# Local attention on 64-row matmul tiles, one score bank per head, with the order of the program redone

## The chip, the cores and the metric

The kernel runs on one core of a Trainium2 chip. The metric is the device time of one execution in microseconds (us); less is better. The engines are named as the profile names them: PE is the matmul engine and PEld its weight loads, DVE, ACT and POOL are the vector, scalar and GpSimd engines, and SP issues the DMAs.

## The reference

Batch 4, 8 heads, 576 positions, 64 channels. Each head gets a full attention over positions averaged by fours, and a local attention in which a position sees only those less than 4 away. Their sum goes through two feed-forward stages.

```python
def _attn_ref(q, k, v):
    ...
    out_d = sm_attn(q_d, k_d, v_d)            # on means of 4 positions
    out_up = np.repeat(out_d, factor, axis=2)
    mask = np.abs(pos[:, None] - pos[None, :]) < factor
    scores = scale * np.matmul(q, k.transpose(0, 1, 3, 2))
    scores = np.where(mask, scores, -1000000000.0)
    scores = scores - np.max(scores, axis=-1, keepdims=True)
    attn = np.exp(scores)
    attn = attn / (np.sum(attn, axis=-1, keepdims=True) + 1e-09)
    out_local = np.matmul(attn, v)
    return (out_up + out_local).astype(np.float32)

def reference(**kwargs):
    ...
    x = np.ascontiguousarray(attn_out.transpose(0, 2, 1, 3)).reshape(B, S, H * D)
    x = _moe_ref(x=x, **moe_kwargs)           # x @ w_in, relu, conv of 3, gate, @ w_out
    return _moe2_ref(x=x, **moe2_kwargs)      # low-rank mix of positions, @ w_ch1, relu, @ w_ch2
```

## The kernel before

The 32 heads are worked off as 16 pairs, two heads of 64 channels on 128 rows. For a pair, q and k are loaded by position (words alq, alk), turned on PE (aqT, akT), and copied out of PSUM by ACT or DVE (aqc, akc). The 576 queries are cut into ten blocks of 58; block i sees the 64 keys that start at KS[i]. Two neighbouring blocks share an instruction's output: block 2j stands on rows 0 to 57, block 2j+1 on rows 64 to 121.

- Scores (emit_S, L449 and L453): one matmul writes the mask into a PSUM tile and one matmul for each block adds q k to it. The tile kbd holds k with the other head's half as zeros, so that 128 rows and 128 moving columns give both heads' scores at once. The five pairs of blocks are split into three (S0) and two (S1), one PSUM tile each.
- Softmax: DVE takes the maxima (emit_M, L460), ACT the exponentials (emit_E, L471), POOL or DVE divides (emit_norm, L514).
- The probabilities are turned on PE (emit_T, L526) and copied into the tile PT (emit_Tc, L542). PT keeps two heads apart and has zeros off its diagonal, so each PSUM tile needs four copies of 64 rows: a head's rows times a block's columns.
- Product with v (emit_PV, L562): for each pair of blocks and each head one matmul over 128 rows, the keys of both blocks, and 116 moving columns. The tile vw holds v by block pair.
- The averaged attention runs beside it (Sd L480, turned probabilities L530, product L573), and emit_x (L594) adds both.

The first feed-forward stage has units of 12 matmuls (g1, L805) and 9 (g2, L867), the second g3 (L974) and g4 (L993); all read pairs of high and low parts. The weights arrive as 64-bit numbers and are decoded (L213 to L220), split (L225) and completed (L229) on ACT, DVE and POOL. Three tiles w1t, in turn, receive the first stage's weights.

Nothing schedules: the string SEQ is the order, a list of words that are emitted one by one. Each engine takes its instructions in that order, so a waiting instruction holds up all behind it on its engine. The PSUM tiles of the attention come from four buffers used in turn (tag "st"). Products of the first stage begin at the word 1.0, when four pairs have gone through; the other pairs are interleaved with the products.

Of the kernel before, what the change touches and what calls it, by code (L numbers as in the profile page):

```python
# [8 lines left out]
F32 = mybir.dt.float32  # L9
# [3 lines left out]
AF = mybir.ActivationFunctionType  # L13
# [8 lines left out]
    SEQ="alk.0 alq.0 alv.0 akT.0 aks.0 aqT.0 aqsv.0 lc C aqc.0 akc.0 wl.0 aS0.0 aS1.0 aM0.0 aE01.0 aM1.0 wd.0 "  # L22
# [143 lines left out]
def mixer_kernel(ctx, tc, q, k, v, w_in, conv_w, w_out, mU, mV, w_ch1, w_ch2, out, stop=9, dbg=None, early_end=False):  # L166
# [5 lines left out]
    nc = tc.nc  # L172
# [106 lines left out]
    for i in range(2):  # L279
        nc.gpsimd.memset(PT[64 * i:64 * i + 64, :, :, 1 - i], 0.0)  # L280

# [787 lines left out]
```

## Time and profile before

| | us |
|---|---|
| median of 3 runs | 804.06 (803.35 to 804.09) |
| the profiled execution | 803.76 |
| its span on the core | 802.0 |
| PE busy | 761.0 (95%) |
| DVE busy | 447.5 (56%) |
| ACT busy | 357.2 (45%) |
| POOL busy | 190.3 (24%) |

The busy shares are means over stages that differ, so the views by stretch of time come first. Matmul records overlap: the time that a group of matmuls takes is read from the start of its row to the start of the next row, not from the mean duration of one. A matmul on 32-bit operands that are not turned leaves two records, so a row with x20 stands for ten matmuls; a transpose or a matmul of the feed-forward stages leaves one.

### The profile page before, as it was taken

The page shows a single profiled execution, that of the slowest core. Times are in us where ns is not written, and L with a number is a line of the kernel's source. Part 1 is how long each engine was busy: PE and PEld are TensorE (multiplying, and loading weights), DVE is VectorE, ACT ScalarE, POOL GpSimd, SP SyncE. Part 2 cuts the span into 40 slices and gives each one's busy share as a digit, 9 for nine tenths or more (in the row PEclk, how much of TensorE's full clock was granted, in tenths as well). Part 3 has the DMA queues.
Part 4 walks back from the last instruction along what each step waited for, and adds up shares of the span by engine and source line. Part 5 has one row for each costly group of instructions (what it writes and reads, how often), then busy time and mean ns, then how long its engine had stood idle before and what let it go on. Part 6 is the DMA issues. An engine that isn't in the chain of part 4 may idle for free.

```text
span 802.0 us, 12065 instructions
## 1 busy us (share of the span) xinstructions
PE 761.0 (95%) x4421; PEld 666.4 (83%) x4421; DVE 447.5 (56%) x879; ACT 357.2 (45%) x1077; POOL 190.3 (24%) x266
## 2 busy tenths in 40 slices
PE   4576999999999999999999999999999999999998
PEld 3455788888888788987899999999999989999997
DVE  6887988788988878898986711121221112122112
ACT  3777887887776665767453311111111111111110
POOL 5356566455415242143610000000000000000000
PEclk9578999999999999999999999999999999999999
DMA  6878564333232113111133210010010001001001
GB/s 153 194 177 197 117 123 95 81 93 101 72 85 74 44 56 103 53 54 54 52 120 121 75 40 0 1 40 1 1 39 1 1 1 40 0 1 40 1 1 39
DMA packets 85967, 50.98 MB, mean 64 GB/s; under 512 B 63228, under 2 KB 80404, under 8 KB 85908
## 3 DMA queue, kind: packets, MB, share of 16 engines
q1 hardware_dynamic: 85908, 50.21, 24.0%
q8 instruction: 35, 0.57, 0.3%
q14 instruction: 24, 0.20, 0.1%
HBM read 45.47 MB, written 4.72 MB: 63 GB/s over the span
## 4 chain that ended last, share of the span: by engine, by line
PE 85%; DVE 7%; ACT 3%; DMA 2%; POOL 1%; issue 1%; SPq 0%; DVEq 0%; POOLq 0%; ACTq 0%
PE acc L993 25%; PE g L974 13%; PE gb L974 13%; PE acc L867 11%; PE g L805 9%; PE S L453 2%; PE gb L805 2%; PE O L562 2%; PE tr L359 1%; DMA w1t<-in_moe_w_out_dram 1%; PE h L901 1%; PE T L526 1%; PE ut L960 1%; PE Sd L480 1%; DVE hc L841 1%
## 5 line engine op out<-in xcount | busy, mean ns | idle before, releaser
L993 PE MATMUL acc<-w,a 128*128 128x512 f32 x864 | 216.6, 394 | 0.0
L993 PEld LDWEIGHTS acc<-w,a 128*128 128x128 f32 x864 | 160.8, 188 | 29.0
L867 PE MATMUL acc<-w,ghl 128*128 128x512 f32 x432 | 117.5, 401 | 0.4 <-DVE ghl L858 0.3
L974 PE MATMUL g<-uT,w 128*128 128x384 f32 x576 | 111.9, 339 | 0.0
L974 PE MATMUL gb<-uT,w 128*128 128x384 f32 x576 | 111.3, 339 | 0.0
L974 PEld LDWEIGHTS gb<-uT,w 128*128 128x128 f32 x576 | 101.9, 188 | 3.8
L974 PEld LDWEIGHTS g<-uT,w 128*128 128x128 f32 x576 | 101.9, 188 | 3.8
L983 DVE SCALAR_TENSOR_TENSOR a<-gb,a 128x384 fp32r<-128x384 f32 x48 | 26.7, 557 | 124.7 <-ACT a L982 124.7
L983 DVE SCALAR_TENSOR_TENSOR a<-g,a 128x384 fp32r<-128x384 f32 x48 | 26.7, 557 | 124.5 <-ACT a L982 124.5
L805 PE MATMUL g<-xhl,w 128*128 128x386 f32 (+1 forms) x456 | 95.2, 347 | 0.0
L867 PEld LDWEIGHTS acc<-w,ghl 128*128 128x128 f32 x432 | 77.6, 188 | 16.5 <-issue 2.5
L982 ACT ACTIVATE a<-g 128x384 fp32r<-128x384 f32 x48 | 23.6, 492 | 136.1 <-PE g L974 127.9
L805 PEld LDWEIGHTS g<-xhl,w 128*128 128x128 f32 x456 | 79.2, 189 | 3.8 <-issue 1.7
L982 ACT ACTIVATE a<-gb 128x384 fp32r<-128x384 f32 x48 | 23.6, 491 | 130.0 <-PE gb L974 126.2
L841 DVE SCALAR_TENSOR_TENSOR hc<-hc,cw 128x384 f32<-128x384 f32 x96 | 65.0, 682 | 11.3 <-ACT hc L835 9.2
L471 ACT ACTIVATE P<-S,nm 122x64 f32<-122x64 f32 x160 | 48.1, 319 | 10.6 <-DVE nm L460 10.4
L858 POOL TENSOR_TENSOR ghl<-hc,ghl 128x384 fp32r<-128x384 f32 x24 | 26.1, 1088 | 83.6 <-ACT ghl L855 73.5
L471 ACT ACTIVATION_READ_ACCUMULATOR P<-S,nm 122x1 f32 x160 | 33.7, 211 | 0.0
L453 PE MATMUL S<-kbd,qT 128*58 128x128 f32 x320 | 28.6, 315 | 5.2 <-DVE kbd L414 5.2
L855 ACT ACTIVATE ghl<-hc 128x384 fp32r<-128x384 f32 x48 | 25.1, 523 | 18.8 <-DVE hc L850 17.1
L850 DVE SCALAR_TENSOR_TENSOR hc<-hc 128x384 f32<-128x384 f32 x48 | 30.3, 633 | 5.6 <-ACT hc L845 5.0
L845 ACT ACTIVATE hc<-hc 128x384 f32<-128x384 f32 x48 | 24.9, 524 | 17.9 <-DVE hc L841 17.7
(131 smaller groups left out, 1076.4 us busy)
## 6 DMA issues: line engine op xcount, KB each, us to landing
wraw<-in_moe_w_ch_dram SPq DMA_DIRECT2D x29, 512.0 KB
kr<-in_k_dram SPq DMA_DIRECT2D x32, 144.0 KB
qr<-in_q_dram SPq DMA_DIRECT2D x32, 144.0 KB
vr<-in_v_dram SPq DMA_DIRECT2D x32, 144.0 KB
out_dram<-u SPq DMA_DIRECT2D x17, 256.0 KB
w1t<-in_moe_w_in_dram SPq DMA_DIRECT2D x8, 512.0 KB
w1t<-in_moe_w_out_dram SPq DMA_DIRECT2D x8, 512.0 KB
vw<-in_v_dram SPq DMA_DIRECT2D x64, 64.0 KB
```

The source lines that it names most:

```text
L453: nc.tensor.matmul(ps[64 * a:64 * a + QB, j], e["qT"][:, QB * i:QB * i + QB], e["kbd"][:, :, KS[i]:KS[i] + W], start=False, stop=j == n - 1)
L471: nc.scalar.activation(out=e["P"][:, i, h], in_=ps[:122, j, h], func=AF.Exp, bias=e["nm"][:, i, h:h + 1], accum_out=e["sm"][:, i, h:h + 1])
L805: nc.tensor.matmul(p[:, :wd], w[:, a, cc], xhl[g, cc][:, b, :wd], start=k == 0, stop=k == 3 * NCC - 1)
L841: nc.vector.scalar_tensor_tensor(out=o, in0=inner(g, hts[n], k), scalar=cw[:, k * NF + f:k * NF + f + 1], in1=o, op0=ALU.mult, op1=ALU.add)
L850: nc.vector.scalar_tensor_tensor(out=o, in0=o, scalar=1.0, in1=inner(g, hts.pop(n), 1), op0=ALU.add, op1=ALU.mult)
L855: nc.scalar.activation(out=t[:, 0], in_=cts[n], func=AF.Copy)
L858: eng.tensor_tensor(ghl[n][:, 1], cts.pop(n), ghl[n][:, 0].bitcast(F32), op=ALU.subtract)
L867: nc.tensor.matmul(acc[g][c], t[:, a, c * P:(c + 1) * P], w[:, b], start=f == 0 and i == 0, stop=f == NF - 1 and i == 2)
L974: nc.tensor.matmul(p[:, :TB], w[:, a, cc], uT[g, cc][:, b, :TB], start=k == 0, stop=k == 3 * NCC - 1)
L982: nc.scalar.activation(out=t[:, 0], in_=p[:, :TB], func=AF.Relu)
L983: nc.vector.scalar_tensor_tensor(out=t[:, 1], in0=p[:, :TB], scalar=0.0, in1=t[:, 0].bitcast(F32), op0=ALU.max, op1=ALU.subtract)
L993: nc.tensor.matmul(acc2[g][c], t[:, a, c * P:(c + 1) * P], w[:, b], start=f == 0 and i == 0, stop=f == NF2 - 1 and i == 2)
```

## The change

- kbd becomes kT: k of both heads on 128 rows without zeros; one copy for a PSUM tile where there were two (emit_kc).
- emit_S makes one PSUM tile for each head (five block pairs by 64 keys). A matmul now uses 64 rows, the head's channels, and 64 moving columns; 20 matmuls a pair where there were 10. emit_M and emit_E go by head.
- PT loses its zeros and its split by head and block: the turned probabilities stand as the transposes left them, a head's keys on 64 rows, and are copied whole (emit_Tc): one copy where there were four.
- emit_PV uses 64 rows and 58 moving columns; 20 matmuls a pair where there were 10. The two heads' outputs stay in one PSUM tile, head 0 on rows 0 to 63 and head 1 on rows 64 to 127. vw is loaded by block, head h on rows 64h and on, with six DMAs a pair in place of eight.
- SEQ is written anew.

```diff
-    SEQ="alk.0 alq.0 alv.0 akT.0 aks.0 aqT.0 aqsv.0 lc C aqc.0 akc.0 wl.0 aS0.0 aS1.0 aM0.0 aE01.0 aM1.0 wd.0 "
+    SEQ="wl.2 wd.2 lc C wd.2 wd.2 wl.0 wd.2 wd.0 wh.2 alk.0 wd.0 wd.0 wd.0 wh.0 alq.0 aqT.0 wo.0 alv.0 avd.0 "
...
-        t = p0.tile([P, 2, S], F32, name=f"kbd{i}")
-        nc.gpsimd.memset(t, 0.0)
-        kbds.append(t)
+        kTs.append(p0.tile([P, S], F32, name=f"kT{i}"))
...
-    PT = pa.tile([P, 2, 5, 2, QB], F32, name="PT")
-    for i in range(2):
-        nc.gpsimd.memset(PT[64 * i:64 * i + 64, :, :, 1 - i], 0.0)
+    PT = pa.tile([P, 5, 122], F32, name="PT")
...
-        vw = st[p]["vw"] = pa.tile([P, 5, 2, D], F32, name="vw", tag="vw")
+        vw = st[p]["vw"] = pa.tile([P, 10, D], F32, name="vw", tag="vw")
...
         for c, src in e["kps"]:
-            for h in range(2):
-                rows = slice(64 * h, 64 * h + 64)
-                engines[h](like(kbd[rows, h, c], src), src[rows])
+            copy(like(e["kT"][:, c], src), src)
...
-        n = SB[m].stop - SB[m].start
-        ps = e["S", m] = ps0.tile([P, n, 2, W], F32, name="S", tag="st")
-        nc.tensor.matmul(ps, identR, mask[:, SB[m]].unsqueeze(2).to_broadcast([P, n, 2, W]), start=True, stop=False)
-        for j in range(n):
+        for h in range(2):
+            e["S", h] = ps0.tile([P, 5, W], F32, name="S", tag="st")
+            nc.tensor.matmul(e["S", h], identR, mask, start=True, stop=False)
+        for j in range(5):
             for a in range(2):
-                i = 2 * (SB[m].start + j) + a
-                nc.tensor.matmul(ps[64 * a:64 * a + QB, j], e["qT"][:, QB * i:QB * i + QB],
-                                 e["kbd"][:, :, KS[i]:KS[i] + W], start=False, stop=j == n - 1)
+                i = 2 * j + a
+                for h in range(2):
+                    rows = slice(64 * h, 64 * h + 64)
+                    nc.tensor.matmul(e["S", h][64 * a:64 * a + QB, j], e["qT"][rows, QB * i:QB * i + QB],
+                                     e["kT"][rows, KS[i]:KS[i] + W], start=False, stop=j == 4)
...
-            for h in range(2):
-                for a in range(2):
-                    (copy2 if a and copy2 else copy)(PT[64 * a:64 * a + 64, h, SB[m], a], src[64 * h:64 * h + 64, :, 64 * a:64 * a + QB])
+            copy(PT[:, SB[m]], ps[:, :122 * n].rearrange("p (i x) -> p i x", i=n))
...
-            c = 2 * QB * (i % 4)
-            for h in range(2):
-                nc.tensor.matmul(O[64 * h:64 * h + 64, c:c + 2 * QB], e["vw"][:, i, h],
-                                 PT[:, h, i].rearrange("p a x -> p (a x)"), start=True, stop=True)
+            for a in range(2):
+                c = 2 * QB * (i % 4) + QB * a
+                for h in range(2):
+                    rows = slice(64 * h, 64 * h + 64)
+                    nc.tensor.matmul(O[rows, c:c + QB], e["vw"][rows, 2 * i + a], PT[rows, i, 64 * a:64 * a + QB],
+                                     start=True, stop=True)
```

Three places show what the new order does. In these rows a number behind the shape counts instructions in a row; L numbers are those of the kernel that the rows are from. First PE among the products, with the scores of one pair (S), turned probabilities (T), products with v (O<-PT) and the averaged attention's (O<-PTd). Before:

```order
L805 MATMUL g<-xhl,w_583 128x386 x12
L449 MATMUL S<-mask,identR 128x384
L453 MATMUL S<-kbd_128,qT_132 58x128 x6
L449 MATMUL S<-mask,identR 128x256
L453 MATMUL S<-kbd_128,qT_132 58x128 x4
L526 MATMUL T<-ident,P 128x122 x3
L530 MATMUL T<-ident,Pd 72x96 x4
L805 MATMUL g<-xhl,w_724 128x386 x6
L867 MATMUL acc<-w_431,ghl 128x512 x3
L562 MATMUL O<-PT,vw 64x116 x2
L867 MATMUL acc<-w_431,ghl 128x512 x6
```

PE among the products now:

```order
L855 MATMUL acc<-w_287,ghl 128x512 x3
L441 MATMUL S<-mask,identR 128x320 x2
L447 MATMUL S<-kT_133,qT_136 58x64 x20
L355 MATMUL tr<-ident,qr 128x96 x3
L520 MATMUL T<-ident,Pd 72x96 x4
L793 MATMUL g<-xhl,w_683 128x386 x6
L355 MATMUL tr<-ident,kr 128x96 x3
L793 MATMUL g<-xhl,w_683 128x386 x6
L855 MATMUL acc<-w_287,ghl 128x512 x3
L355 MATMUL tr<-ident,kr 128x96 x3
L551 MATMUL O<-PT,vw 64x58 x20
L562 MATMUL O<-PTd,vd 64x144 x4
```

A pair's scores are one group of 20 small matmuls behind both masks, where they were two groups with a mask ahead of each, and its products with v are here one group of 20, followed by the averaged attention's, which keep 72 rows.

Second, ACT before the products begin: the copies of the turned probabilities (PT), of k (kbd, kT), exponentials (P, Pd) and weights (w1t, w). Before:

```order
L471 ACTIVATE P,sm<-S,nm 122x64 x6
L213 ACTIVATE w1t<-w1t 128x512
L542 COPY PT<-T 64x3x58 x4
L471 ACTIVATE P,sm<-S,nm 122x64 x2
L225 ACTIVATE w_360<-w1t 128x512
L471 ACTIVATE P,sm<-S,nm 122x64 x2
L213 ACTIVATE w1t<-w1t 128x512
L414 COPY kbd_128<-tr 64x576 x2
```

ACT before the products now:

```order
L407 COPY kT_133<-tr 128x576
L489 ACTIVATE Pd,smd<-Sd,nmd 96x144 x3
L461 ACTIVATE P,sm<-S,nm 122x64 x2
L529 COPY PT<-T 128x366
L376 ACTIVATE qT_136<-tr 128x576
L213 ACTIVATE w1t<-w1t 128x512
L225 ACTIVATE w_658<-w1t 128x512
```

Four copies of 64 rows have become one of 128, and two copies of k have become one.

Third, the first DMAs that SP issues: k, q and v of the first pairs (kr, qr, vr) and weights (w1t, craw). Before:

```order
L298 DMA kr<-in_k_dram 96x6x64 x2
L298 DMA qr<-in_q_dram 96x6x64 x2
L320 DMA vr<-in_v_dram 72x2x256 x2
L700 DMA craw<-in_moe_conv_w_dram 24x256
L329 DMA w1t<-in_moe_w_in_dram 128x4x256
L327 DMA w1t<-in_moe_w_out_dram 128x1024
```

SP's first DMAs now:

```order
L325 DMA w1t<-in_moe_w_in_dram 128x4x256
L688 DMA craw<-in_moe_conv_w_dram 24x256
L325 DMA w1t<-in_moe_w_in_dram 128x4x256
L295 DMA kr<-in_k_dram 96x6x64 x2
L295 DMA qr<-in_q_dram 96x6x64 x2
L316 DMA vr<-in_v_dram 72x2x256 x2
```

Two weight blocks of 512 KB now stand ahead of the first pair's k and q.

## Rows read from the trace of the kernel before

**Rows 1.** Stretches: busy us (instructions) by engine, PEclk, DMA share, GB/s.

```profile
core 0: us, PE busy (x) PEld busy (x) DVE busy (x) ACT busy (x) POOL busy (x), PEclk, DMA share, GB/s
0.00:88.00 88.00, 55.39 (x410) 44.18 (x410) 70.75 (x136) 61.40 (x227) 47.34 (x76) 0.79 0.75 176
93.00:280.00 187.00, 186.83 (x1397) 156.10 (x1398) 159.15 (x373) 141.16 (x520) 89.25 (x134) 1.00 0.35 84
280.00:400.00 120.00, 115.70 (x571) 101.99 (x570) 105.42 (x172) 77.58 (x164) 46.46 (x50) 1.00 0.20 62
400.00:802.00 402.00, 398.30 (x2020) 359.99 (x2018) 108.06 (x188) 72.09 (x142) 5.79 (x4) 1.00 0.08 28
```

**Rows 2.** Chain that ended last, front: start us, us, what.

```profile
60.09 4.60 DMA w1t<-in_moe_w_out_dram
...
70.86 6.59 DMA w1t<-in_moe_w_out_dram
```

**Rows 3.** Waits of the DMA queue, 0 to 88 us: total, times, longest.

```profile
SPq L327 <- POOL w L229: 16.3, 4, 7.8
```

**Rows 4.** Timeline of PE, untiled and score matmuls: start us, us, instruction.

```profile
118.95 0.87 PE L453 MATMUL S<-kbd,qT 128*58 128x128 f32 x12
119.75 0.39 PE L449 MATMUL S<-mask,identR 128*128 128x256 f32 x1
120.07 0.65 PE L453 MATMUL S<-kbd,qT 128*58 128x128 f32 x8
120.65 0.53 PE L526 MATMUL T<-ident,P 122*128 122x122 f32 x3
...
241.10 0.37 PE L526 MATMUL T<-ident,P 122*128 122x122 f32 x2
241.31 0.33 PE L530 MATMUL T<-ident,Pd 96*72 96x96 f32 x2
```

**Rows 5.** Timeline of PE, products with v and their neighbours.

```profile
123.21 0.42 PE L562 MATMUL O<-PT,vw 128*64 128x116 f32 x4
123.56 1.66 PE L867 MATMUL acc<-w,ghl 128*128 128x512 f32 x6
...
155.31 1.77 PE L805 MATMUL g<-xhl,w 128*128 128x388 f32 x9
157.00 1.21 PE L562 MATMUL O<-PT,vw 128*64 128x116 f32 x20
158.14 0.47 PE L359 MATMUL tr<-ident,kr 96*128 96x96 f32 x3
...
212.83 0.42 PE L562 MATMUL O<-PT,vw 128*64 128x116 f32 x4
213.08 0.71 PE L573 MATMUL O<-PTd,vd 72*64 72x144 f32 x8
```

**Rows 6.** Chain that ended last, late: twelve products in a row.

```profile
493.46 2.10 PE g L974 x12
```

**Rows 7.** Timeline of the weight loads at one group's start, two windows.

```profile
157.00 0.14 PEld L562 LDWEIGHTS O<-PT,vw 128*64 128x64 f32 x2 [0.26 <-ACT ghl L855]
...
157.00 0.20 PEld L562 LDWEIGHTS O<-PT,vw 128*64 128x64 f32 x4 [0.26 <-ACT ghl L855]
```

**Rows 8.** Groups by line: busy us, mean ns of one, idle before.

```profile
L542 ACT COPY PT<-T 64x174 f32<-64x174 f32 (+1 forms) x74 | 20.4, 276 | 7.9 <-PE T L526 4.0 <-PE T L530 2.2 <-DVE PT L542 0.9
L542 DVE COPY PT<-T 64x116 f32<-64x116 f32 (+1 forms) x54 | 16.4, 303 | 1.4 <-ACT PT L542 0.4 <-PE T L526 0.3
...
L414 ACT COPY kbd<-tr 64x288 f32<-64x288 f32 (+1 forms) x29 | 13.6, 468 | 6.1 <-PE tr L359 5.6 <-DVE ks L424 0.4
...
L414 DVE COPY kbd<-tr 64x288 f32<-64x288 f32 (+1 forms) x23 | 11.3, 491 | 1.8 <-ACT kbd L414 1.6
```

**Rows 9.** Groups by line and shape: the nearest copies in width.

```profile
L546 ACT COPY PTd<-T 72x384 f32<-72x384 f32 x10 | 4.7, 469 | 0.9 <-PE T L530 0.9
...
L546 ACT COPY PTd<-T 72x192 f32<-72x192 f32 x9 | 2.8, 315 | 0.2
```

More of the change, by code (lines that the diff above doesn't have):

```diff
@@ L264, in mixer_kernel @@
         nc.vector.tensor_copy(mask[rows, c0:c0 + n], mtmp[rows, i].unsqueeze(1).to_broadcast([64, n, W]))
-    kbds, qdbds, qTs = [], [], []
+    kTs, qdbds, qTs = [], [], []
     for i in range(2):
-        t = p0.tile([P, 2, S], F32, name=f"kbd{i}")
-        nc.gpsimd.memset(t, 0.0)
-        kbds.append(t)
+        kTs.append(p0.tile([P, S], F32, name=f"kT{i}"))
         t = p0.tile([P, 3, 96], F32, name=f"qdbd{i}")
@@ L304, in load_vw @@
         b, cc = divmod(p, NCC)
-        vw = st[p]["vw"] = pa.tile([P, 5, 2, D], F32, name="vw", tag="vw")
+        vw = st[p]["vw"] = pa.tile([P, 10, D], F32, name="vw", tag="vw")
         for h in range(2):
-            a = v[b, 2 * cc + h]
-            nc.sync.dma_start(vw[:W, 0, h], a[:W])
-            nc.sync.dma_start(vw[64:, 4, h], a[S - W:])
-            for t, i in ((vw[:W, 1:], 2), (vw[64:, :4], 1)):
-                nc.sync.dma_start(t[:, :, h], bass.AP(tensor=a.tensor, offset=a.offset + KS[i] * D,
-                                                      ap=[[D, W], [2 * QB * D, 4], [1, D]]))
+            a, t = v[b, 2 * cc + h], vw[64 * h:64 * h + 64]
+            nc.sync.dma_start(t[:, 0], a[:W])
+            nc.sync.dma_start(t[:, 9], a[S - W:])
+            nc.sync.dma_start(t[:, 1:9], bass.AP(tensor=a.tensor, offset=a.offset + KS[1] * D,
+                                                 ap=[[D, W], [QB * D, 8], [1, D]]))
     def load_vr(p):
@@ L403, in emit_qsum, with emit_kc @@
         e["qd"] = qd
-    def emit_kc(p, *engines):
+    def emit_kc(p, copy):
         if not 0 <= p < NPAIR:
@@ L409, in emit_kc @@
         e = st[p]
-        kbd = e["kbd"] = kbds[p % 2]
+        e["kT"] = kTs[p % 2]
         for c, src in e["kps"]:
-            for h in range(2):
-                rows = slice(64 * h, 64 * h + 64)
-                engines[h](like(kbd[rows, h, c], src), src[rows])
+            copy(like(e["kT"][:, c], src), src)
     def emit_ksum(p):
@@ L436, in emit_vd, with emit_S @@
         e["vd"] = vd
-    def emit_S(p, m):
+    def emit_S(p):
         if not 0 <= p < NPAIR:
@@ L442, in emit_S, with emit_M, emit_E @@
         e = st[p]
-        if "P" not in e:
-            e["P"] = pa.tile([122, 5, 2, W], F32, name="P", tag="P", bufs=2)
-            e["nm"] = pa.tile([122, 5, 2], F32, name="nm", tag="nm", bufs=2)
-            e["sm"] = pa.tile([122, 5, 2], F32, name="sm", tag="sm", bufs=2)
-        n = SB[m].stop - SB[m].start
-        ps = e["S", m] = ps0.tile([P, n, 2, W], F32, name="S", tag="st")
-        nc.tensor.matmul(ps, identR, mask[:, SB[m]].unsqueeze(2).to_broadcast([P, n, 2, W]), start=True, stop=False)
-        for j in range(n):
-            for a in range(2):
-                i = 2 * (SB[m].start + j) + a
-                nc.tensor.matmul(ps[64 * a:64 * a + QB, j], e["qT"][:, QB * i:QB * i + QB],
-                                 e["kbd"][:, :, KS[i]:KS[i] + W], start=False, stop=j == n - 1)
-    def emit_M(p, m):
+        e["P"] = pa.tile([122, 5, 2, W], F32, name="P", tag="P", bufs=2)
+        e["nm"] = pa.tile([122, 2, 5], F32, name="nm", tag="nm", bufs=2)
+        e["sm"] = pa.tile([122, 5, 2], F32, name="sm", tag="sm", bufs=2)
+        for h in range(2):
+            e["S", h] = ps0.tile([P, 5, W], F32, name="S", tag="st")
+            nc.tensor.matmul(e["S", h], identR, mask, start=True, stop=False)
+        for j in range(5):
+            for a in range(2):
+                i = 2 * j + a
[3 more added lines that the diff above has]
+                                     e["kT"][rows, KS[i]:KS[i] + W], start=False, stop=j == 4)
+    def emit_M(p, h):
         if not 0 <= p < NPAIR:
             return
-        nc.vector.tensor_reduce(out=st[p]["nm"][:, SB[m]], in_=st[p]["S", m][:122], op=ALU.max,
-                                axis=AX.X, negate=True)
-    def emit_E(p, m, part=None):
+        nc.vector.tensor_reduce(out=st[p]["nm"][:, h], in_=st[p]["S", h][:122], op=ALU.max, axis=AX.X, negate=True)
+    def emit_E(p, h, part=None):
         if not 0 <= p < NPAIR:
@@ L466, in emit_E @@
         e = st[p]
-        ps = e["S", m]
-        for j in range(SB[m].stop - SB[m].start) if part is None else (part,):
-            for h in range(2):
-                i = SB[m].start + j
-                nc.scalar.activation(out=e["P"][:, i, h], in_=ps[:122, j, h], func=AF.Exp,
-                                     bias=e["nm"][:, i, h:h + 1], accum_out=e["sm"][:, i, h:h + 1])
+        for i in range(5) if part is None else (part,):
+            nc.scalar.activation(out=e["P"][:, i, h], in_=e["S", h][:122, i], func=AF.Exp,
+                                 bias=e["nm"][:, h, i:i + 1], accum_out=e["sm"][:, i, h:h + 1])
     def emit_Sd(p):
@@ L538, in emit_Tc @@
             n = SB[m].stop - SB[m].start
-            src = ps[:, :122 * n].rearrange("p (i x) -> p i x", i=n)
-            for h in range(2):
-                for a in range(2):
-                    (copy2 if a and copy2 else copy)(PT[64 * a:64 * a + 64, h, SB[m], a], src[64 * h:64 * h + 64, :, 64 * a:64 * a + QB])
+            copy(PT[:, SB[m]], ps[:, :122 * n].rearrange("p (i x) -> p i x", i=n))
         if m:
@@ L559, in emit_PV @@
         for i in (range(0, 4), range(4, 5))[half]:
-            c = 2 * QB * (i % 4)
-            for h in range(2):
-                nc.tensor.matmul(O[64 * h:64 * h + 64, c:c + 2 * QB], e["vw"][:, i, h],
-                                 PT[:, h, i].rearrange("p a x -> p (a x)"), start=True, stop=True)
+            for a in range(2):
[4 more added lines that the diff above has]
+                                     start=True, stop=True)
     def emit_PVd(p):
@@ L672, in mixer_kernel @@
         "qT0": (4, lambda p: transposes(p, "q", 0)), "qT1": (4, lambda p: transposes(p, "q", 1)),
-        "kc": (3, lambda p: emit_kc(p, A, A)), "kv": (3, lambda p: emit_kc(p, V, V)),
-        "km": (3, lambda p: emit_kc(p, A, V)), "ks": (3, emit_ksum),
+        "kc": (3, lambda p: emit_kc(p, A)), "kv": (3, lambda p: emit_kc(p, V)), "ks": (3, emit_ksum),
         "qc": (4, emit_qc), "qv": (4, lambda p: emit_qc(p, True)), "qs": (4, emit_qsum), "qsv": (4, lambda p: emit_qsum(p, "DVE")), "qsa": (4, lambda p: emit_qsum(p, "ACT")),
@@ L686, in mixer_kernel @@
         if m < 2:
-            OPS[f"S{m}"] = 2, lambda p, m=m: emit_S(p, m)
             OPS[f"M{m}"] = 2, lambda p, m=m: emit_M(p, m)
             OPS[f"E{m}"] = 2, lambda p, m=m: emit_E(p, m)
-            for j in range(3 - m):
+            for j in range(5):
                 OPS[f"E{m}{j}"] = 2, lambda p, m=m, j=j: emit_E(p, m, j)
+    OPS["S"] = 2, emit_S
     NK = conv_w.shape[0]
```

280 rows, old and new, of the table SEQ are left out of this document.

## The prediction

> **What bounds the kernel now.** I read the stretches first [rows 1]. They show two kernels in one. From 93 us on, PE is busy 186.83 of 187 us, then 115.70 of 120, then 398.30 of 402, at a granted clock of 1.00: whatever PE has to do there is the time. In the first 88 us PE is busy 55.39 us at a mean granted clock of 0.79, and no engine is full: DVE 70.75, ACT 61.40, POOL 47.34, DMA share 0.75 at 176 GB/s. The chain of waits passes there through weight loads of 4.60 and 6.59 us [rows 2], and SP's queue stands 16.3 us behind POOL's last step on a weight [rows 3], because a w1t tile is loaded again only then. So the front is a chain of latencies over full-ish engines. The sum therefore has two terms: PE's work after the first product, where each ns counts, and the length of the front.
>
> At the first product both orders have done the same attention: scores of 6 pairs, turned probabilities and products with v of 4 (counted in the order's rows). So 10 pairs of scores and 12 of products with v are left among the products in both, and the first term is a comparison of like with like.
>
> **What a small matmul costs now.** Two turned probabilities of 122 columns take 241.31 - 241.10 = 0.21 us, 105 ns a record, 0.86 ns a column [rows 4]. Scores: 12 records of 128 columns take 119.75 - 118.95 = 0.80 us, 8 take 120.65 - 120.07 = 0.58; four more cost 0.22, 55 ns a record, half of 128 x 0.86 = 110. The two blocks of a pair, on 58 array columns each, thus already run side by side. Products with v likewise: x20 takes 1.14, x4 takes 0.35 [rows 5], 16 more cost 0.79, 49 ns a record, half of 116 x 0.85. What stays over is 0.80 - 12 x 0.055 = 0.14 for a group of scores and 0.35 - 4 x 0.049 = 0.15 for one of products with v. Where a group with the same 64 columns follows (212.83 to 213.08) x4 takes 0.25, not 0.35, so 0.10 of that is the way back to the whole array. The way in costs too: nine products ahead of such a group take 157.00 - 155.31 = 1.69, and at 2.10/12 = 0.175 [rows 6] they would take 1.58. An excursion into small tiles costs 0.11 + 0.14 = 0.25 us.
>
> **The change part by part, on PE among the products.**
> Scores: 200 matmul records of 128 columns become 400 of 64, which cost 64 x 0.86 = 55 ns where alone. Now: 200 x 55 = 11.0 us. If all four (two heads' rows, two blocks' columns) run side by side: 100 x 55 = 5.5. If only the columns do, as now: 200 x 55 = 11.0. No row shows row halves side by side; every attention matmul of before spans at least 72 rows. I take 5.5, since the change gives each head its own bank and nearest is the row in which column halves do it fully. **-5.5 us**, ends 0 and -5.5.
> The Trainium skill (TensorE: Matmul & The Clock Gate, Part 3, Packing small matmuls) has row and column tiles run concurrently and reports 10.6 times for 16 tiles; by it the term is -5.5.
> Products with v: 240 records of 116 columns become 480 of 58, with the heads on the diagonal, so two side by side as now. Now 240 x 49 = 11.8. A pass of 58 columns is 58 x 0.85 = 49 ns, 240 x 49 = 11.8; but each pass needs its own weights, and the loads show that two finish 0.06 after the two before them [rows 7]. That is hidden behind 99 ns and sticks out behind 49. Between 49 and 60 I take 57: 13.7. **+1.9 us**, ends 0 and +2.6.
> Excursions: 47 before, 27 now (scores 20 groups to 10, products with v 22 to 18, and these stand next to each other more often): -20 x 0.25 = -5.0. But the averaged attention's product keeps 72 rows, so a step between it and PV, free before, is now a change of tiling, 12 times. Between 0.10 (the way back) and 0.25 I take 0.20: +2.4. **-2.6 us**, ends -3.8 and -2.0. Three transposes of k fall into the front: 3 x 0.08 = -0.2.
> Sum: -5.5 + 1.9 - 2.6 - 0.2 = **-6.4**.
>
> **On the other engines.** PT: 74 copies of 20.4 us on ACT and 54 of 16.4 on DVE [rows 8] become 25 and 7, 366 or 244 columns wide. The nearest are 384 columns at 469 ns and 192 at 315 [rows 9], so about 0.46 and 0.36: 16 x 0.46 + 16 x 0.36 = 13, **-24 us** of work. Copies of k: 13.6 + 11.3 us in 52 copies become 26, **-12**. Among the products this hides: ACT and DVE are busy 141 and 159 of 187 us there [rows 1], and PE waits for neither, so I cost it at nothing; were DVE to become late it would be worth at most PE's idle 120 - 115.7 = 4.3 us between 280 and 400.
> In the front it is on the chain. Up to the first product I count, with the traced durations, ACT 58 for 65 us, DVE 67 for 69, POOL 40 for 45; part of it is a weight and three quarters less decoded there (52 decode steps for 59), which the later stretch must take on. In all 8% less work; 8% of 88 us is 7. DVE, the fullest, loses 3%: 2 us. Against it, the first k and q come behind two weight blocks of 512 KB: 1.05 MB at 176 GB/s is 6 us in which the attention can't begin, though the decode can. Bytes are the same otherwise. From -7 to +6 I take **-4**: work falls on every engine, and the decode fills the first microseconds.
>
> **The forecast.** 803.8 - 6.4 - 4 = **793.4 us** for the execution profiled at 803.76; the median of the runs, 804.06, is the same within 0.3. The ends of the terms give 803.8 - 9.5 - 7 = 787 and, with row halves overlapping and the front unchanged, 803.8 - 5.1 = 799.
>
> **Rivals.**
> 1. Row halves do not overlap. Scores stay at 11.0, products with v become 480 x 57 = 27.4 for 11.8, +15.6; with -2.8 for excursions and transposes +12.8 among the products, and -4 in front: **813, slower**. For it: no row shows the overlap. Against: column halves overlap fully. It decides if head 1's matmul starts only when head 0's ends. Chance 0.08.
> 2. Only the products with v lose the overlap, because the two row halves write one bank. -5.5 + 15.6 - 2.8 - 4: **807, slower**. Chance 0.06. Against it, the two heads lie on different rows of that bank.
> The Trainium skill (PSUM — Partial Sum Buffer, PSUM bank collisions raise a hardware error) says that different row tiles can't access one bank at the same time, while column tiles on other partitions can; no run here shows either.
> 3. The front pays for its new beginning, +6 instead of -4: **803, no change**. Chance 0.10, which I split 0.03 faster, 0.05 same, 0.02 slower.
> 4. The scores of a pair now take two of the four PSUM buffers at once and hold them until ten exponentials are through, and PE's queue stops at the next user. At 1 us for each of 10 pairs it eats the gain: **803**; chance 0.06 (0.01, 0.02, 0.03). For it: four buffers in turn. Against: between 93 and 280 us PE waits 0.2 us in all, and before held two as well.
> 5. The front shrinks with its whole work, -7, and PE's idle 4.3 us between 280 and 400 loses 3 with DVE's lighter load: 803.8 - 6.4 - 10 = **787**, faster. Chance 0.12.
>
> **How the numbers follow.** The forecast has 0.58. 0.2% (1.6 us) is about what a measurement of this kernel can tell from no change. Faster: 0.58 + 0.12 + 0.03 + 0.01 = 0.74. Same: 0.05 + 0.02 = 0.07. Slower: 0.08 + 0.06 + 0.02 + 0.03 = 0.19. The likeliest case alone spans 787 to 799. The range of 8 in 10 goes from 784, where rival 5 is mostly in, to 808, which takes in rivals 2, 3 and 4 and leaves out rival 1.
>
> **What would show it.** In the profile after: 40 score records between two masks and the next group should take about 10 x 0.055 + 0.14 = 0.7 us (1.25 if only columns overlap); 40 records of products with v about 20 x 0.057 + 0.15 = 1.3 us (2.4 if the heads follow one another); the row of v's followed by the averaged attention's should show a step. The first product should start near 84 us, and PE should be busy throughout from about 89 us. PE waits on the attention's PSUM tiles beyond 1 us would make rival 4 right. The prediction is wrong above all if the start of the products moves by more than the PE work saved.

## The result and the profile after

The changed kernel takes **791.52 us** (median of 4 runs, 791.23 to 794.56) against 803.7 us for the kernel before (4 runs, 802.65 to 804.09): ratio 0.986, interval 0.983 to 0.989, 12.2 us less. The profiled execution took 791.73 us with a span of 789.5. The forecast was 793.4. The sum has two terms, and neither came out at its size; the total is near because their misses have opposite signs.

Stretches of the kernel after, read as [rows 1] (busy us and instructions by engine, then PEclk, DMA share, GB/s):

```profile
core 0: us, PE busy (x) PEld busy (x) DVE busy (x) ACT busy (x) POOL busy (x), PEclk, DMA share, GB/s
0.00:88.00 88.00, 57.37 (x699) 49.05 (x700) 70.09 (x146) 61.12 (x233) 43.53 (x73) 0.81 0.84 186
93.00:280.00 187.00, 184.24 (x1795) 160.64 (x1790) 148.08 (x329) 134.62 (x481) 75.44 (x114) 0.99 0.35 87
280.00:400.00 120.00, 116.86 (x581) 103.35 (x580) 106.78 (x184) 77.05 (x166) 34.39 (x38) 1.00 0.20 62
400.00:789.50 389.50, 385.76 (x1956) 348.20 (x1954) 94.65 (x164) 65.94 (x131) 11.66 (x9) 1.00 0.08 26
```

PE is still the time after the first product, but no longer without a gap: 184.24 of 187 us where it was 186.83. DVE and ACT have lost 11 and 7 us in that stretch; the DMA share of the front is up from 0.75 to 0.84. The first product now starts at 79.6 us (88.0 before), and from its start to the end of the last product it is 706.2 us (710.3 before). So the front gave **8.4 us** and the products' stretch **4.1**. PE's row of the first product and the whole stretch, first before, then after:

```profile
88.00 2.38 PE L805 MATMUL g<-xhl,w 128*128 128x386 f32 x12
...
88.00:798.29 710.29, 705.61 (x4014) 622.18 (x4012) 376.01 (x741) 295.83 (x851) 142.93 (x191) 1.00 0.18 49
```

```profile
79.60 3.16 PE L793 MATMUL g<-xhl,w 128*128 128x386 f32 x12
...
79.60:785.82 706.22, 699.83 (x4451) 624.00 (x4450) 359.92 (x702) 289.15 (x819) 127.27 (x169) 1.00 0.18 50
```

PE is busy 5.8 us less in the stretch and idle 1.7 us more (6.4 for 4.7).

PE's timeline of the kernel after, one group of scores and two pairs' products with v (to be held against [rows 4, 5]):

```profile
105.40 1.38 PE L551 MATMUL O<-PT,vw 64*64 64x58 f32 x40
106.71 0.72 PE L562 MATMUL O<-PTd,vd 72*64 72x144 f32 x8
...
183.35 0.79 PE L447 MATMUL S<-kT,qT 64*58 64x64 f32 x40
184.07 0.47 PE L355 MATMUL tr<-ident,qr 96*128 96x96 f32 x3
...
209.19 0.44 PE L551 MATMUL O<-PT,vw 64*64 64x58 f32 x8
209.56 0.72 PE L562 MATMUL O<-PTd,vd 72*64 72x144 f32 x8
210.21 1.14 PE L551 MATMUL O<-PT,vw 64*64 64x58 f32 x32
211.28 0.43 PE L516 MATMUL T<-ident,P 122*128 122x122 f32 x2
```

A pair's 40 score records take 184.07 - 183.35 = 0.72 us. Products with v: 40 records in a row take 106.71 - 105.40 = 1.31, 32 take 1.07 and 8 take 0.37, so 24 cost 0.70, 58 ns for two. The step from 8 of them to the averaged product (0.37) costs 0.37 - 4 x 0.058 = 0.14, where it was 0.25 - 4 x 0.049 = 0.05 [rows 5]: 0.09 more.

Copies of the turned probabilities (PT) and of k in the kernel after, groups by line over the first 300 us (busy us, mean ns), answering [rows 8]:

```profile
L529 ACT COPY PT<-T 128x366 f32<-128x366 f32 (+1 forms) x25 | 10.4, 419 | 7.3 <-PE T L520 5.9 <-PE T L516 1.3
L407 ACT COPY kT<-tr 128x288 f32<-128x288 f32 (+1 forms) x18 | 8.1, 460 | 4.9 <-DVE ks L417 4.9
...
L407 DVE COPY kT<-tr 128x288 f32<-128x288 f32 (+1 forms) x8 | 4.2, 525 | 4.8 <-PE tr L355 4.8
L529 DVE COPY PT<-T 128x244 f32<-128x244 f32 (+1 forms) x7 | 3.0, 425 | 1.9 <-PE T L520 1.9
```

61.7 us of copies have become 25.7. The longest new wait of PE in the stretch is at a load of v:

```profile
169.72 0.44 PE L551 MATMUL O<-PT,vw 64*64 64x58 f32 x6
171.81 1.25 PE L551 MATMUL O<-PT,vw 64*64 64x58 f32 x34 [1.65 <-DMA vw<-in_v_dram]
```

Between 174 and 176 us, behind it, the granted clock is 0.50, the lower of the two levels (1.2 GHz); over 172 to 178 us it is 0.72 in the mean, and over the first 2.4 us of the products 0.64. An estimate from these shares: 6 x 0.28 + 2.4 x 0.36 = 2.5 us lost.

```profile
174.00:176.00 2.00, 2.00 (x8) 1.69 (x8) 1.68 (x7) 0.36 (x1) 0.00 (x0) 0.50 0.62 143
```

### The profile page after: what moved, and what is told of

It is laid out like the page before. It is cut to its first block, busy times and chain, and to the rows that moved or that the text cites. A ratio compares the mean times of both kernels' runs of the same rounds, so it can differ in the third digit from the quotient of the medians.

```text
span 789.5 us, 13123 instructions
## 1 busy us (share of the span) xinstructions
PE 749.0 (95%) x5061; PEld 665.2 (84%) x5061; DVE 423.5 (54%) x830; ACT 343.7 (44%) x1029; POOL 168.3 (21%) x237
## 4 chain that ended last, share of the span: by engine, by line
PE 84%; DVE 8%; ACT 3%; DMA 2%; SPq 1%; issue 1%; POOL 1%; DVEq 0%; POOLq 0%; ACTq 0%
PE acc L981 25%; PE gb L962 13%; PE g L962 13%; PE acc L855 11%; PE g L793 9%; PE O L551 3%; PE gb L793 2%; PE tr L355 2%; PE Sd L470 1%; DVE hc L829 1%; PE O L562 1%; PE T L516 1%; PE h L889 1%; PE ut L948 1%; DMA qr<-in_q_dram 1%
## 5 line engine op out<-in xcount | busy, mean ns | idle before, releaser
L855 PE MATMUL acc<-w,ghl 128*128 128x512 f32 x432 | 112.8, 399 | 0.1
L855 PEld LDWEIGHTS acc<-w,ghl 128*128 128x128 f32 x432 | 80.1, 190 | 17.1 <-DVE ghl L846 1.4
L793 PE MATMUL g<-xhl,w 128*128 128x386 f32 (+1 forms) x456 | 92.9, 346 | 0.2 <-ACT hc L804 0.2
L793 PEld LDWEIGHTS g<-xhl,w 128*128 128x128 f32 x456 | 80.5, 191 | 2.9 <-issue 0.7
L551 PEld LDWEIGHTS O<-PT,vw 64*64 64x64 f32 x640 | 23.5, 149 | 12.4 <-DVE xd L572 2.7
L551 PE MATMUL O<-PT,vw 64*64 64x58 f32 x640 | 27.1, 237 | 7.0 <-DVE xd L572 2.4
```

What stands on the lines that cost most here:

```text
L551: nc.tensor.matmul(O[rows, c:c + QB], e["vw"][rows, 2 * i + a], PT[rows, i, 64 * a:64 * a + QB], start=True, stop=True)
L793: nc.tensor.matmul(p[:, :wd], w[:, a, cc], xhl[g, cc][:, b, :wd], start=k == 0, stop=k == 3 * NCC - 1)
L855: nc.tensor.matmul(acc[g][c], t[:, a, c * P:(c + 1) * P], w[:, b], start=f == 0 and i == 0, stop=f == NF - 1 and i == 2)
```

## The experiments

All start from the changed kernel, except the last, which starts from the kernel before. "First product" is the start of the first row of L793 (or its counterpart) in PE's timeline, "stretch" the time from there to the end of the last product; both are of the one profiled execution, which lies up to 2.2 us from the median.

| kernel | median us | ratio to before, interval | first product | stretch |
|---|---|---|---|---|
| before | 803.7 | 1 | 88.0 | 710.3 |
| changed | 791.5 | 0.986 (0.983 to 0.989) | 79.6 | 706.2 |
| e1 scores on 128 rows | 796.1 | 0.991 (0.989 to 0.992) | 82.1 | 707.9 |
| e2 v on 128 rows | 791.0 | 0.985 (0.983 to 0.986) | 80.6 | 705.1 |
| e3 old order | 808.1 | 1.005 (1.003 to 1.008) | 88.4 | 712.0 |
| e4 copies in parts | 809.9 | 1.008 (1.006 to 1.010) | 84.5 | 719.1 |
| e5 first pair first | 793.8 | 0.987 (0.984 to 0.989) | 83.3 | 704.9 |
| e6 four loads of v early | 805.0 | 1.002 (1.000 to 1.004) | 81.0 | 718.4 |
| e7 only PT in parts | 802.3 | 0.999 (0.997 to 1.001) | 83.0 | 711.8 |
| e8 v of pair 9 earlier | 792.1 | 0.985 (0.983 to 0.987) | 82.2 | 704.4 |
| e9 e8, and xd of pair 3 on ACT | 790.5 | 0.985 (0.983 to 0.987) | 78.4 | 706.4 |
| e10 old front, new rest | 799.4 | 0.996 (0.994 to 0.997) | 90.9 | 704.8 |
| e11 decode back in the front | 797.6 | 0.991 (0.988 to 0.994) | 85.8 | 706.9 |
| e12 before, less decode in front | 806.4 | 1.003 (1.002 to 1.004) | 87.1 | 714.1 |

**How far a single front can be trusted.** Up to 150 us e8 has exactly the changed kernel's order, yet its first product comes 2.6 us later. Among the first differences is a load of q; PE's timeline, first of the changed kernel, then of e8:

```profile
10.79 1.20 PE L355 MATMUL tr<-ident,qr 96*128 96x96 f32 x6 [4.39 <-DMA qr<-in_q_dram]
```

```profile
11.28 1.20 PE L357 MATMUL tr<-ident,qr 96*128 96x96 f32 x6 [4.89 <-DMA qr<-in_q_dram]
```

Half a microsecond is between them at 11 us and 2.6 us at the end of the front; that the one grows into the other is not shown. I read nothing from fronts that differ by less than 3 us. Stretches repeat no better than to 2 us: e5 has the changed kernel's order behind the first product and takes 704.9 for 706.2 us there, and e8 and e9, again of one order there, 704.4 and 706.4. e5's stretch has no lower clock in it, and its PE is busy 697.80 us:

```profile
83.27:788.17 704.90, 697.80 (x4452) 621.73 (x4450) 360.92 (x702) 289.77 (x821) 127.96 (x169) 1.00 0.18 50
```

### Do the matmul tiles overlap? (e1, e2)

e1 lets the score matmuls read all 128 rows, e2 the products with v:

```diff
-                    rows = slice(64 * h, 64 * h + 64)
+                    rows = slice(0, P)
```

```diff
-                    nc.tensor.matmul(O[rows, c:c + QB], e["vw"][rows, 2 * i + a], PT[rows, i, 64 * a:64 * a + QB],
+                    nc.tensor.matmul(O[rows, c:c + QB], e["vw"][:, 2 * i + a], PT[:, i, 64 * a:64 * a + QB],
```

> The changed kernel, but each score matmul reads all 128 rows of q and k instead of its head's 64, so the two heads' scores are summed (the output is then not the reference's); instructions, columns, banks, copies and order are those of the changed kernel. Theory (row halves run side by side): a pair's 40 score records take 20 x 0.056 + 0.15 = 1.27 us instead of 0.72; 10 pairs lie among the products, so the time grows by 5.5 to 6 us over the changed kernel's 791.5, to about 797. Rival (the gain comes from the new order and the fewer copies, not from row halves): no change, 791 to 792.

> The changed kernel, but each product with v reads all 128 rows of v and of the turned probabilities, so a head's output also holds the other head's keys (not the reference's output). Theory (in these products the heads run side by side because they write different columns of the array; row halves give nothing): 40 records take 1.31 us as now, the time stays within 1 us of 791.5. Rival (the row halves are what lets them overlap): 40 records take 2.4 us, 12 pairs among the products, +13 us, 804.

e1's scores in PE's timeline:

```profile
102.29 1.38 PE L447 MATMUL S<-kT,qT 128*58 128x64 f32 x40
103.60 0.47 PE L355 MATMUL tr<-ident,qr 96*128 96x96 f32 x3
```

1.31 us for the 40 records that take 0.72 on 64 rows: 0.59 for each of ten pairs is 5.9 us, and the median rose by 4.6, near the theory. The profiled stretch rose by only 1.7: e1's has no lower clock in it, where the changed kernel lost some 2.5 us to it. It is the rows that show it: row halves overlap, four tiles at a time. That bears out the Trainium skill (TensorE: Matmul & The Clock Gate, Part 3, Packing small matmuls), which has row and column tiles run concurrently. Products with v, e2:

```profile
106.28 1.54 PE L551 MATMUL O<-PT,vw 128*64 128x58 f32 x40
107.65 0.71 PE L562 MATMUL O<-PTd,vd 72*64 72x144 f32 x8
...
209.43 0.45 PE L551 MATMUL O<-PT,vw 128*64 128x58 f32 x8
209.71 0.71 PE L562 MATMUL O<-PTd,vd 72*64 72x144 f32 x8
```

1.37 us against 1.31 on 64 rows (1.21 against 1.30 at the two later places with 40 in a row), and the time is the same: the theory held. The heads overlap by their array columns and gain nothing from their rows. Eight records ahead of the averaged product take 0.28 here for 0.37 in the changed kernel: with more than 64 rows on both sides the 0.09 of the step is gone. The Trainium skill (PSUM — Partial Sum Buffer, PSUM bank collisions raise a hardware error) says that different row tiles can't access one bank at the same time. Here the two heads' tiles, different in rows and in columns, write one bank on different partitions, and 24 of their records take 0.70 us on 64 rows as on 128 (e2), so no time is lost to it.

### Tiles or order? (e3, e10)

e3 keeps the tiles and takes the old SEQ, mapped word for word. e10 takes the old SEQ up to the first product and the new one from there, with the eight words that the old front had not done put at its start (words of SEQ):

```diff
-wl.2 wd.2 lc C wd.2 wd.2 wl.0 wd.2 wd.0 wh.2 alk.0 wd.0 wd.0 wd.0 wh.0 alq.0
...
+alk.0 alq.0 alv.0 akT.0 aks.0 aqT.0 aqsv.0 lc C aqc.0 akc.0 wl.0 aS.0
...
```

> The tiles of the changed kernel, its matmuls, copies and exps, in the order of the kernel before (the one eviction word that no longer exists dropped, the exps of a two-block word standing one behind the other, everything else where it stood). Theory A (the tiles carry the gain, the new order only the start): the stretch from the first product on keeps its 4 us, and the front falls back to the 88 us of before less what shorter copies give there, so 795 to 800 us with the first product at 84 to 88 us. Rival B (the gain needs the order that was made for these durations): 803 us or more, with new waits of TensorE among the products. Rival C (the order does nothing): 790 to 793 us.

> The tiles of the changed kernel; up to the first product the order of the kernel before (as in the run of the old order), from there on the new order, with the ten words that the old front had already done left out of it and the eight that it had not done put at its start. Old order throughout gave 808.1 us with the first product at 88.4 us; the changed kernel 791.5 with it at 79.6. Theory A (the new order saves in both places, some 9 us in the front and some 6 behind the first product, where the old one makes TensorE wait): first product at 87 to 89 us, the stretch behind it back at 704 to 707 us, together 798 to 801.5 us. Rival B (the front alone carries it, and the waits behind it follow from the late start): 805 us or more. Rival C (the rest alone carries it): 795 us or less.

e3: 808.1 us, 4 us **slower than before**. Theory B held, and more than B said: the front is back at 88.4 too. Its matmuls are the changed kernel's, but between 93 and 280 us PE stands:

```profile
93.00:280.00 187.00, 180.61 (x1826) 154.84 (x1825) 146.34 (x326) 128.66 (x478) 89.94 (x134) 1.00 0.34 83
```

6.4 of 187 us are idle, 0.2 before [rows 1]. PE's waits behind e3's first product are many and short; the largest that before has not is for exponentials (total, times, longest):

```profile
PE O L560 <- ACT P L470: 2.4, 3, 1.4
```

e10 splits the two: with the new order behind the first product the stretch is 704.8 again, with the old front the first product is at 90.9 (2 us beyond theory A), and the time is 799.4, as theory A had it. So on the same tiles the new order is worth 7.9 us in the front (799.4 to 791.5) and 8.7 behind it (808.1 to 799.4) by the medians; the profiled stretches give 7.2 for the latter (712.0 to 704.8).

What the new order does in the front is plain in the first 40 us: PEclk, DMA share and GB/s are the last three numbers. Before, changed, e3 and e10:

```profile
0.00:40.00 40.00, 20.81 (x115) 16.89 (x116) 30.07 (x53) 22.17 (x79) 17.52 (x39) 0.76 0.75 173
```

```profile
0.00:40.00 40.00, 21.99 (x244) 18.52 (x245) 28.28 (x59) 24.58 (x92) 17.32 (x38) 0.79 1.02 211
```

```profile
0.00:40.00 40.00, 19.88 (x204) 16.07 (x206) 29.04 (x55) 21.77 (x82) 16.62 (x36) 0.77 0.78 183
```

```profile
0.00:40.00 40.00, 19.89 (x198) 16.35 (x200) 28.85 (x55) 21.40 (x80) 16.33 (x36) 0.96 0.79 177
```

The kernels with the old start move 173 to 183 GB/s there and reach the first product at 87 to 91 us; all with the new start move 203 to 211 and reach it at 78 to 86. Up to the first product the changed kernel moves 191 GB/s x 79.6 us = 15.2 MB, the kernel before 176 x 88 = 15.5. Nearly the same bytes come sooner. No run raised the rate by itself, so that the rate is the cause is a reading.

### What in the front (e5, e11, e12)

```diff
+alk.0 alq.0
 wl.2 wd.2 lc C wd.2 wd.2 wl.0 wd.2 wd.0 wh.2
-alk.0
 wd.0 wd.0 wd.0 wh.0
-alq.0
 aqT.0
```

> The changed kernel with the loads of k and q of the first pair put at the very start of the program, ahead of the products' first weights; nothing else moves. Theory A (the start with weights costs the first pair's chain, as the prediction's third rival had it, and the front was shorter for other reasons): the first product earlier by 2 to 6 us, 786 to 790 us. Rival B (the weights are what the front waits for, so they belong first): the first product later by 1 to 4 us, 792.5 to 796 us. Rival C (the two loads are not bound, the queue has room): within 1 us of the changed kernel.

e5 does not tell much: 793.8 us, and its front is 3.7 us later, little above what equal fronts differ by. Both numbers lie in the ranges of rival B, but its interval overlaps the changed kernel's. Theory A is not borne out, since nothing came earlier; between B and C it stays open.

e11 puts ten words of the old front back (wl.14, wd.13 four times, wd.14 three times, wh.13 and the last step of weight 12; wl.13 moves up too):

```diff
 px.0.2
+wl.13
 alk.6 wd.11
...
 ac1.3
+wd.13
 akc.6 akT1.6
...
 aks.6 wo.11
+wl.14
 and.4
+wd.13
 aPd.3 axdv.3
+wd.13
 aPVb.3
+wd.13
 aSd.5 alk.7
+wd.14
...
 pX.0.3
-wl.13
 1.0
-wd.13 wd.13
 1.0 1.0 1.0
```

> The changed kernel with the seven decode steps of weights 13 and 14, the load of 14 and the two steps that complete 13 put back ahead of the first product, as the kernel before had them, spread over the last third of the front; nothing else moves. They are about 4.5 us of DVE work and 1 us of ScalarE's. Theory A (the front is a queue on DVE, so what is taken out of it shortens it): first product 3 to 5 us later, 794 to 796.5 us. Rival B (the front waits for other things, and the new arrangement of the words, not the seven steps less, is what shortened it): first product within 1.5 us, 790.5 to 793.5 us.

(The two steps that it calls those that complete 13 are the last of 12 and the first of 13's completion.) 797.6 us, first product 6.2 us later: more than theory A's 3 to 5, and not by its mechanism. DVE is busy 62.0 us up to e11's first product and 62.8 up to the changed kernel's, so no queue on DVE has grown. The chain that ended last in e11's front (start, us, what) shows the place:

```profile
65.72 0.23 SPq L325
...
66.48 8.15 DMA kr<-in_k_dram
...
79.22 4.01 DMA w1t<-in_moe_w_in_dram
...
83.31 0.66 ACT w1t L215
```

A weight's load stands ahead of k on SP's queue and waits there behind POOL's steps; k is issued only then and takes 8.15 us. Later ACT stands before the first decode step of the next weight until that has landed, with exponentials behind it. ACT's waits for such loads, e11 up to 85.8 us and the changed kernel up to 79.6 (total, times, longest):

```profile
ACT w1t L215 <- DMA w1t<-in_moe_w_in_dram: 11.4, 4, 5.5
```

```profile
ACT w1t L213 <- DMA w1t<-in_moe_w_in_dram: 6.9, 3, 2.6
```

e12 does the reverse in the kernel before, and takes the same ten words out of its front:

```diff
 ac1.3
-wd.13
 aT2.3 ac2.3
...
 axd.3
-wd.13 wd.13
 aks.6 akv.6
-wo.12
 aS0.5 Z akT1.6
-wd.13 wl.14 wd.14 wd.14
 aEd.4 px.0.2
-wh.13
 an.4 alw.3 aPVb.3
-wd.14
 aM0.5
...
 1.0 aM1.5
+wd.13
 1.0
+wd.13
 1.0 1.0
+wo.12
...
```

> The kernel before, its tiles and its order kept, with one thing of the new order: the seven decode steps of weights 13 and 14, the load of 14, the step that completes 12 and the first that completes 13 stand behind the first product instead of ahead of it, spread among the first three units; weight 15 moves back behind them. In the changed kernel the same steps put back into the front made the first product 6 us later and the time 6 us longer. Theory A (this decode work is the larger part of what the front lost, with either tiles): first product 3 to 6.5 us earlier than 88.0, the stretch behind it within 1.5 us of 710, together 798 to 801.5 us. Rival B (the old tiles' copies bind the front on ScalarE instead, so the decode steps were not what it waited for): first product within 1.5 us of 88 and 802 to 805 us. Rival C (the steps hold DVE and ScalarE among the products, where the old tiles leave less room): the front shorter, but the stretch longer by 3 us or more, and 802 us or more.

806.4 us: rival B in the front, only 0.9 us earlier, which is less than equal fronts differ by, and rival C behind it, 3.8 us more stretch. In the old front these steps were not what was waited for; that the old tiles' order has less room for them behind it is rival C's reading. So the same words, where I put them, cost 6 us in the new front and nothing in the old one.

### Are the copies free? (e4, e7)

e4 cuts the copies again, PT in four and k in two, e7 only PT; everything else stays:

```diff
-            copy(PT[:, SB[m]], ps[:, :122 * n].rearrange("p (i x) -> p i x", i=n))
+            for h in range(2):
+                for a in range(2):
+                    copy(PT[64 * h:64 * h + 64, SB[m], 64 * a:64 * a + QB], src[64 * h:64 * h + 64, :, 64 * a:64 * a + QB])
...
-            copy(like(e["kT"][:, c], src), src)
+            for h in range(2):
+                copy(like(e["kT"][64 * h:64 * h + 64, c], src[64 * h:64 * h + 64]), src[64 * h:64 * h + 64])
```

> The changed kernel, but the turned probabilities are copied in four parts and k in two, as in the kernel before (same values). Theory (the copies are on the chain in the front and hidden among the products): the first product starts 3 to 5 us later than at 79.5 us, the time grows by 3 to 5 us, to 795 to 797, and PE waits no longer among the products. Rival A (the front is shorter because of its order alone): no change, 791 to 792. Rival B (the copies matter among the products too): more than 8 us, 800.

> The changed kernel with only the copies of the transposed probabilities cut into four (per head and row of blocks), k copied whole. With both in parts the time was 809.9 us, 18.4 us above the changed kernel, 4.9 us of it ahead of the first product. Theory A (TensorE waits behind ScalarE in proportion to the copy work added, 12.6 us of ScalarE's 20.6 us from these copies): 801 to 805 us, with the new waits of TensorE spread among the products. Rival B (cutting k holds the chain to the scores, which stands earlier, and does most of it): 792 to 797 us. Rival C (either cut alone upsets the order as much as both): 807 us or more.

809.9 us, 18.4 above the changed kernel, as rival B had it; with PT alone 802.3, 10.8 above, as theory A of e7 had it. The copies of e4 by line:

```profile
L534 ACT COPY PT<-T 64x174 f32<-64x174 f32 (+1 forms) x100 | 23.0, 279 | 5.8 <-PE T L522 3.7 <-PE O L556 0.8 <-PE T L518 0.7
L409 ACT COPY kT<-tr 64x288 f32<-64x288 f32 (+1 forms) x36 | 16.1, 448 | 5.3 <-DVE ks L419 3.9 <-PE tr L355 1.0
```

With DVE's 15.1 us they are 54.2 us for 25.7: 28.5 us more work on two engines makes the stretch 12.8 us longer and the front 4.9. ACT is not full: 143.60 of 187 us. But PE stands, in many short waits; e4 between 84 and 280 us (total, times, longest):

```profile
PE g L798 <- ACT hc L809: 2.1, 4, 0.8
PE tr L355 <- DVE PTd L538: 1.9, 1, 1.9
PE S L443 <- ACT PTd L538: 1.3, 1, 1.3
```

```profile
93.00:280.00 187.00, 176.29 (x1745) 150.20 (x1746) 146.79 (x337) 143.60 (x540) 79.57 (x113) 0.99 0.35 83
```

PE is idle 10.7 of 187 us. In the kernel before 61.7 us of the same copies held PE up for 0.2 us in that stretch [rows 1, 8]. So it seems that the order around the copies sets what they cost; no run has them in parts in another order on the same tiles.

### The wait at 170 us (e6, e8, e9)

Four words alw stand directly ahead of their products. e6 moves all four behind the products of the pair before, e8 only that of pair 9, by some 25 words; e9 adds to e8 that the copy xd of pair 3, for which PE stands 2.4 us at 76 us, goes from DVE to ACT (e9's edit; e8 has the part from alv.10 on):

```diff
 and.4 aPd.3
-axdv.3
+axd.3
 aPVb.3
...
 r1.10 c0.10 alv.10
+alw.9
 c1.10 th.10
...
 gh.11 gL.11
-alw.9
 aPVa.9 aPVb.9
```

> The changed kernel with one kind of word moved: the loads of v by block for pairs 5, 9, 12 and 15, which the order puts right in front of the products that read them, go right behind the products of the pair before, which free their tile. Theory (PE's 1.7 us wait at 170 us and the granted clock of one half that follows it are a cost of the new order): the wait goes, 2 us and up to 1.7 us of clock, so 788 to 790. Rival (the wait only moves to the next tile that is not ready): 791 to 792.

> The changed kernel with the three-part load of v of pair 9, which stands directly ahead of its products and behind a load that waits for ScalarE, put some 25 words earlier, behind the load of that pair's averaged v; nothing else moves. Theory A (the wait of 1.9 us at 170 us is SyncE's place in its queue, and the stretch at a granted clock of 0.5 behind it its echo): the wait is gone and the time 1.5 to 4 us less, 787.5 to 790 us. Rival B (as where four such loads were moved, what stands behind them on SyncE's queue comes later and costs more than is won): 793 us or more, with a new wait of TensorE elsewhere. Rival C: no change, because the wait's place is taken by another.

> The load of v of pair 9 placed earlier as in the run before, and the copy xd of pair 3, for which TensorE stands 2.4 us at 76 us (its release is a copy that DVE does last of eleven in a row), given to ScalarE, which is between exponentials there. Theory A (that stand is a queue on DVE, and the products start when the chain behind it is through): the stand shrinks to under 1 us and the first product comes 1 to 2 us earlier; with the 1.8 us that the earlier load saves behind the first product, 787 to 789.5 us. Rival B (DVE's chain is the front, with or without this copy, or ScalarE is no better): no more than the load's part, 789.5 to 792 us.

e6: 805.0 us, neither theory. SP issues in its order. In e6 it waits 4.9 us for the products that free vw, and a weight's load stands behind that; it is issued at 101.86, in the changed kernel at 93.39:

```profile
96.76 0.47 SPq L307 DMA_DIRECT2D vw<-in_v_dram  x1
...
101.86 0.43 SPq L325 DMA_DIRECT2D w1t<-in_moe_w_out_dram  x1
```

```profile
93.39 0.45 SPq L323 DMA_DIRECT2D w1t<-in_moe_w_out_dram  x1
```

ACT stands 7.3 us for this weight, until its first decode step at 107.57, and PE behind ACT's hc for 5.1 (e6, ACT's and PE's timeline):

```profile
107.57 0.66 ACT L215 ACTIVATE w1t<-w1t 128x512 f32<-128x512 f32 x1 [7.30 <-DMA w1t<-in_moe_w_out_dram]
```

```profile
108.67 1.66 PE L795 MATMUL g<-xhl,w 128*128 128x386 f32 x4 [5.09 <-ACT hc L806]
```

A late load of v held PE for 1.65 us; here a late weight stops ACT's whole queue. e8 leaves the other loads in place: the wait is gone, as theory A says, and the granted clock between 174 and 176 us is 1.00:

```profile
174.00:176.00 2.00, 1.74 (x32) 1.27 (x28) 1.63 (x5) 2.00 (x11) 0.00 (x0) 1.00 0.98 183
```

But the median, 792.1, is not lower, as rival C has it, and the stretch, 1.8 us shorter, differs by no more than equal ones do. Nor does such a wait bring the lower clock by itself. e5 has the same wait at the same load (e2 too, 1.57 us), and its clock stays at 1.00 behind it:

```profile
175.19 1.25 PE L553 MATMUL O<-PT,vw 64*64 64x58 f32 x34 [1.52 <-DMA vw<-in_v_dram]
...
175.00:181.00 6.00, 5.81 (x69) 5.24 (x70) 4.25 (x13) 2.06 (x8) 1.26 (x1) 1.00 0.80 156
```

e9 has no such wait left, and its clock falls elsewhere, to 0.72 in the mean between 362 and 368 us. At 76 us PE stands 0.4 us instead of 2.4 in e9, the first product is at 78.4, the median 790.5, in the range of rival B. Its interval, 0.983 to 0.987, overlaps the changed kernel's, so it is the lowest median measured but not shown to be faster.

## Why the prediction was right, step by step

- **What bounds the kernel:** right. The front and PE's work behind the first product are the two terms, in every run of the table.
- **Scores, -5.5:** right. 0.72 us a pair for the 0.7 foretold, and e1 gives back 5.9 us by its rows. Rival 1 is out.
- **Products with v, +1.9:** right. 58 ns for two records where 57 were taken. Rival 2 is out.
- **Excursions, -2.6:** mis-sized. The step to the averaged product, taken at 0.20 twelve times, costs 0.09: +1.1 in place of +2.4. With that the sum of the term is -7.7.
- **The term as a whole, -6.4:** the trace of the changed kernel gives -4.1, in three parts. PE's busy time where the clock stays up (e5) is 7.8 us under before, close to the -7.7. The changed kernel is busy 2.0 us longer than e5, which goes with its lower clock at two places, and PE is idle 1.7 us more than before; the wait for v, 1.65 us, is the longest new one. The prediction has PE "busy throughout" at the full clock and puts both at nothing.
- **The copies, "I cost it at nothing":** the step that failed, in its reason. Against the kernel before it stands, since PE waits 0.2 us of 187 there and lighter copies had no more to win. But it asked only whether the engines have room, 141 and 159 of 187 us, and e4 shows 12.8 us of PE's time in the same copies with ACT busy 143.60 of 187. That the new order is built on the lighter copies and has no cover to spare is a reading.
- **The front, -4:** the right sign at half its size (-8.4, with 3 us of play). "Work falls on every engine" is not enough as the reason: in e3 ACT and DVE are busy 53.70 and 65.69 us up to the first product, for 61.40 and 70.75 before [rows 1], and it starts at 88.4. "The decode fills the first microseconds" agrees with the DMA rate of the first 40 us. The two weight blocks ahead of k and q (rival 3) cost nothing that e5 could show.
- **Tiles and order as separate terms:** the sum treated the -6.4 as the tiles' and the -4 as the order's. e3 shows that the tiles alone make the kernel 4 us slower, and e10 that the order behind the first product is worth 7 to 9 us. The number came out because the order goes with the tiles, so that their PE time was really saved, and by luck: 2.3 us too much in the stretch stand against 4.4 too little in the front.
- **Rival 4** (scores hold two PSUM buffers): out; PE waits for no score tile in the stretch. **Rival 5** had the front's size about right, but PE's idle between 280 and 400 fell only from 4.3 to 3.1 us.

What stays open: what the old order's front waits for instead (e12 says only that it isn't these decode steps), whether weights first or k and q first matters, what the new order would give the old tiles (not run as a whole), and why the clock falls behind some gaps and not behind others of the same length.

## What to carry to other kernels

When tiles and a hand-written order change together, ask what the new tiles would do in the old order and the old tiles in the new one; a saving on PE is only a saving if the order keeps PE fed. An engine that is a quarter idle can still cost the bound engine time (e4); these runs suggest that the distance between a copy and its reader hides it, not the busy share. Before a load is moved up, look at what stands behind it on its queue, and at which engine will stand in front of the load that comes late.

## What I had not expected of the hardware

- Four 64-row tiles (two row halves, two column halves) take 0.72 us for 40 records, about 57 ns for four behind 0.15 us of start; with two column halves alone (128 rows) the same 40 take 1.31.
- Products of 58 columns take 58 ns for two records on 64 rows (0.70 us for 24); a record of 116 columns, which does the work of two of these, took 49 ns [rows 5]. That the weight loads are the bound is the prediction's reading of [rows 7]; no run here took them away.
- The same instructions in the same order reach the end of an 80 us front 2.6 us apart, after a load of q that PE waited for 0.5 us longer at 11 us.
- One gap of 1.65 us in PE's work was followed by 2 us and more at a granted clock of 0.50; in e5 and e2, with gaps of 1.52 and 1.57 us at the same load, the clock stayed at 1.00.
